# Attention and MLP on one core: the opening of the kernel rearranged (first keys and queries in float32, value rows once per half batch, an immediate cosine shift)

## The chip, the cores and the metric

One Trainium2 chip; the kernel runs on one core. A time is the device time of one execution in microseconds (us). The kernel before took 355.42, 353.09 and 354.77 us in three runs, median 354.77. The engines are TensorE (PE, with its weight loads PEld), VectorE (DVE), ScalarE (ACT), GpSimd (POOL) and SyncE (SP, which here only issues DMAs). Each works its own instructions in program order and waits for the others by semaphores.

## The reference

Attention with a sliding window and global tokens, and behind it an MLP:

```python
batch, heads, seq, head_dim = 8, 8, 576, 64        # 8 global tokens, drawn from 0..575
scores = q @ k.T / 8
mask   = (|i - j| <= 32) or i is global or j is global
attn   = softmax(where(mask, scores, -1e9)) @ v      # per batch and head
x      = attn.transpose(0, 2, 1, 3).reshape(4608, 512)
h      = x @ w_in                                    # 512 x 2048
out    = (h * cos(h)) @ w_out                        # 2048 x 512, float32
```

The inputs are float32; the kernel computes in fp16 with float32 sums. A flag that the kernel computes on the way decides at the end if a slow general path runs as well; with these inputs it does not.

## The kernel before, in words

**Units.** Two heads make a *pair* (numbers 0 to 31), two pairs a *half batch* (0 to 15), two half batches a batch. Pairs 0 to 9 (`2 * HY`) are done in the *opening*, by functions with their own layout of five blocks of 120 keys; pairs 10 to 31 run beside the MLP. The MLP has 9 tiles of 512 tokens; a tile can start when its batch's attention is done.

**Order.** Nothing is scheduled by a planner: `tc.manual_schedule()` keeps the program's order on each engine. Strings of steps spell it: `FRONT` for the opening, then `MID`, `FIFTH`, `SIXTH` and `ORDER` for half batches 4 on. A step is a letter with a number. In `FRONT`: `k3`, `q3` turn keys and queries of pair 3 (`local_k`, `local_q`); `s3` its scores and exponentials (`scores5`); `p3` its values (`values5`); `x3` turns its result into the MLP's input `xT` (`turn_x5`); `C1` casts the values of half batch 1 (`cast_vn`, on GpSimd); `y` makes their global value rows; `L2` loads keys and queries of half batch 2; `E0`, `E1` gather the global rows of keys and queries of the later pairs, `H0` casts and `H1` turns them, `g4` copies them into pair 4's buffers; `f2`, `w4` are filler matmuls on TensorE; `W` and `O` load the MLP's weights, `K5` casts half batch 5 to fp16 in DRAM, `m` and `t` are the first MLP products and cosines.

**A pair in the opening.** Keys lie in SBUF with eight tokens a partition. TensorE transposes them (16 small transposes, L595), and for pairs below 4 (`PK`) also picks out the 8 global tokens by products with a 0/1 selector (`one_k`, `one_q`, L312). ScalarE copies both from PSUM (L313, L604; for queries L313, L615, L616). TensorE makes scores (L631), ScalarE the exponentials in four pieces (L634 twice, L638 twice), VectorE multiplies by the mask `mask5` (L635 twice, L639 once), TensorE multiplies by the values (L646), VectorE divides by the row sums (L660 to L666), TensorE turns the result (L678) and VectorE copies it to `xT` (L679 to L684).

**Values.** Rows of v come in float32 by SyncE's queue into `vn32`, are cast by GpSimd (L402) into `vw`; TensorE sums the 8 global rows by a selector `one_v` (L409), and ScalarE copies them into the first 8 partitions of each of the five blocks (L410). In the kernel before this is done once per pair (`y0.0`, `y0.1`, ...): 8x640 elements a copy. Steps `M1` to `M4` clear the edge of the next half batch's buffer on VectorE (L378) and load it.

**First loads.** SyncE loads the indices of the global tokens three times in different layouts (L237 to L239) and then values. GpSimd's queue loads keys and queries and casts them to fp16 on the way (`load_qk`, L279): pair 0, pair 1, then whole half batches. VectorE builds the window mask's band (`build_band`, L475 to L485), the selectors (`build_ones`, L304, L305) and the mask (`build_mask5`, L498 to L519).

**MLP.** A tile is 16 times four matmuls (L762), a cosine on ScalarE with a per-partition shift `pio2` (L768), a product on VectorE (L769), and 16 groups of four output matmuls (L800).

Of the kernel before, what the change touches and what calls it, by code (L numbers as in the profile page):

```python
# [9 lines left out]
FP32 = mybir.dt.float32  # L10
# [45 lines left out]
FRONT = ("M1 s0 E0 C0 E1 L2 k1 q1 w4 s1 y0.0 f4 k2 q2 C1 H0 p0 M2 L3 y0.1 s2 k3 q3 f2 x0 p1 M3 H1 g4 g5 g6 C2 y1.0 s3 g7 L4 I k4 q4 f2 x1 p2 M4 y1.1 s4 "  # L56
         "C3 W0 k5 q5 f2 x2 p3 y2.0 s5 g8 g9 W1 W2 W3 k6 q6 f2 x3 p4 y2.1 s6 C4 Y0 k7 q7 f2 x4 p5 n0 y3.0 s7 k8 q8 f2 x5 p6 y3.1 s8 H2 k9 q9 f2 x6 p7 y4.0 s9 "
         "x7 p8 y4.1 O m m x8 K5 p9 t t + m m t t x9 -")
# [146 lines left out]
def kernel(  # L205
# [31 lines left out]
    nc.sync.dma_start(gidx_all, dview(gi, 0, (0, P), (1, 2 * G)))  # L237
    nc.sync.dma_start(gidx_col, dview(gi, 0, (0, 16), (2, G), (1, 1)))
    nc.sync.dma_start(gidx_row, dview(gi, 0, (2 * G, 1), (1, 2 * G)))  # L239
# [67 lines left out]
    def pick_globals(pr, t, src, ones, n, to):  # L307
# [5 lines left out]
        nc.scalar.copy(to, view(t, (0, to.shape[1]), (1, G)))  # L313
# [61 lines left out]

    def next_values(s):

        nc.vector.memset(vn_of(s)[0:64, 0], 0.0)  # L378
        load_vn(s)
# [18 lines left out]
    def cast_vn(s):  # L398
        if s > 1:
            nc.gpsimd.tensor_copy(gate, pm_of[max(pm_of)][0:1, 2 * CN - 1 : 2 * CN])  # L400
# [3 lines left out]
    def value_rows(s, part):  # L404

        hs = slice(2 * part, 2 * part + 2)
        rows = ps.tile([P, 512], FP32, tag="h", bufs=2, name="rows")
        for t in range(NK5):
            nc.tensor.matmul(rows[0:G, 0 : 2 * D], one_v[:, t], vn16(s)[:, t, hs, 0:D], start=t == 0, stop=t == NK5 - 1)  # L409
        nc.scalar.copy(vn16(s)[0:G, :, hs, 0:D], view(rows[0:G], (0, NK5), (D, 2), (1, D)))  # L410
# [187 lines left out]
    def local_k(pr):  # L598
        to = kw[pr % NK][:, :, G:]
        if pr < 2 * HY:  # L600
            t, g = turned(kn[pr // 2 % NN], pr, KP)
            if pr < PK:
                pick_globals(pr, g, kn[pr // 2 % NN], one_k, KP, k5(pr)[:, :, 0:G])
            nc.scalar.copy(k5(pr)[:, :, G:].rearrange("p n (j r) -> p n j r", r=RW),  # L604
                           view(t, (KS // RW, NK5), (1, KS // RW), (QP, RW)))
# [3 lines left out]
    def local_q(pr):  # L609
        to = qb[pr % NK][:, :, G:]  # L610
        if pr < 2 * HY:
            t, g = turned(qn[pr // 2 % NN], pr, QP)
            if pr < PK:
                pick_globals(pr, g, qn[pr // 2 % NN], one_q, QP, q5(pr)[:, 1:, 0:G])
# [474 lines left out]
```

## Time and profile before

| quantity | value |
|---|---|
| runs, median of 3 | 354.77 us (353.09 to 355.42) |
| the profiled execution: span from first to last instruction | 353.2 us |
| the profiled execution's own time around it | not listed apart; the runs' median is 1.6 us above the span |
| TensorE busy | 332.5 us, 94% |
| VectorE, ScalarE, GpSimd busy | 71%, 70%, 31% |
| granted TensorE clock, mean | 0.983 |
| first exponential of pair 0 | 10.85 us |
| second group of MLP products starts | 56.58 us |

The page gives busy times per engine; they are averages over stages with different limits. The timeline lists instructions by start time, with "xN" for N like ones in a row and in brackets how long the engine had been idle before and what ended that. The windows give busy time per engine within a stretch.

### The profile page before, as it was taken

The page shows a single profiled execution, that of the slowest core. Times are in us where ns is not written, and L with a number is a line of the kernel's source. Part 1 is how long each engine was busy: PE and PEld are TensorE (multiplying, and loading weights), DVE is VectorE, ACT ScalarE, POOL GpSimd, SP SyncE. Part 2 cuts the span into 40 slices and gives each one's busy share as a digit, 9 for nine tenths or more (in the row PEclk, how much of TensorE's full clock was granted, in tenths as well). Part 3 has the DMA queues.
Part 4 walks back from the last instruction along what each step waited for, and adds up shares of the span by engine and source line. Part 5 has one row for each costly group of instructions (what it writes and reads, how often), then busy time and mean ns, then how long its engine had stood idle before and what let it go on. Part 6 is the DMA issues. An engine that isn't in the chain of part 4 may idle for free.

```text
span 353.2 us, 8389 instructions
## 1 busy us (share of the span) xinstructions
PE 332.5 (94%) x3169; PEld 170.9 (48%) x3169; DVE 250.1 (71%) x611; ACT 245.9 (70%) x423; POOL 108.5 (31%) x221
## 2 busy tenths in 40 slices
PE   7887789999986999999999999999999999999993
PEld 3566675444443444544444545454544444444442
DVE  6565888887586778778787979697878466556410
ACT  8778987884754877777878787777878856644300
POOL 8854847434070507050705071416000100000000
PEclk9898989999999999999999999999999999999998
DMA  5999993999999999999999999999980000100112
GB/s 82 186 149 165 167 192 41 207 164 132 165 147 160 146 199 135 178 118 194 143 187 139 183 139 176 135 161 153 179 93 32 31 32 30 60 32 30 58 63 68
DMA packets 165891, 44.58 MB, mean 126 GB/s; under 512 B 153764, under 2 KB 160996, under 8 KB 165668
## 3 DMA queue, kind: packets, MB, share of 16 engines
q1 hardware_dynamic: 105860, 26.70, 51.2%
q0 software_dynamic: 59984, 17.28, 50.5%
q8 instruction: 27, 0.44, 0.5%
q14 instruction: 20, 0.16, 0.2%
HBM read 44.41 MB, written 19.17 MB: 180 GB/s over the span
## 4 chain that ended last, share of the span: by engine, by line
PE 73%; ACT 8%; DVE 5%; DMA 5%; issue 4%; SPq 3%; POOL 1%; ACTq 0%; POOLq 0%; DVEq 0%
PE po L800 32%; PE ph L762 30%; PE tx L744 2%; DMA kn<-in_k_dram 2%; PE st L699 2%; ACT e L702 2%; PE pv L719 2%; ACT e L634 1%; DMA vw<-vg 1%; ACT e L707 1%; SPq L414 1%; PE po L782 1%; ACT e L638 1%; DVE xn L666 1%; DVE pm L639 1%
## 5 line engine op out<-in xcount | busy, mean ns | idle before, releaser
L762 PE MATMUL ph<-xT,w_in 128*128 128x512 f16 x576 | 140.3, 379 | 1.1 <-DVE g L769 0.3
L768 ACT ACTIVATE cos<-ph,pio 128x512 f16<-128x512 f32 x144 | 97.1, 687 | 62.1 <-PE ph L762 59.9
L800 PE MATMUL po<-w_out,g 128*128 128x512 f16 x560 | 135.4, 379 | 0.0
L769 DVE TENSOR_TENSOR g<-cos,ph 128x512 f16<-128x512 f16 x144 | 95.9, 685 | 42.9 <-ACT cos L768 41.7
L762 PEld LDWEIGHTS <-w_in 128*128 128x128 f16 x576 | 54.2, 97 | 64.6 <-issue 4.6
L800 PEld LDWEIGHTS <-g 128*128 128x128 f16 x560 | 53.7, 98 | 63.6
L703 DVE TENSOR_TENSOR pm<-e,mask 128x512 f16<-128x512 f16 x44 | 18.8, 426 | 19.0 <-ACT e L702 17.7
L702 ACT ACTIVATE e<-st 128x512 f16<-128x512 f32 x44 | 23.9, 594 | 10.0 <-PE st L699 9.8
L980 POOL COPY gate<-xn 1x1 f16<-1x1 f16 x8 | 1.4, 180 | 87.9 <-DVE xn L730 87.9
L752 POOL COPY xT<-xg 128x4 f16 x48 | 15.6, 325 | 32.5 <-DVE xT L747 29.9
L272 POOL DMA_DIRECT2D q<-in_q_dram x11 | 24.0, 2182 | 0.0
L818 ACT ACTIVATE xn<-xn 128x1536 f16<-128x1536 f16 (+1 forms) x16 | 22.5, 1407 | 0.0
L730 DVE TENSOR_TENSOR xn<-pv,r_all 128x768 f16<-128x768 f32 x22 | 21.1, 958 | 1.0
L805 ACT COPY o<-po 128x512 f32<-128x512 f32 x17 | 10.0, 586 | 14.7 <-PE po L800 14.3
L807 DVE COPY o<-po 128x512 f32<-128x512 f32 x18 | 12.4, 690 | 9.0 <-PE po L800 8.5
L272 POOL DMA_DIRECT2D k<-in_k_dram x11 | 18.1, 1645 | 0.9 <-issue 0.9
L768 ACT ACT_TABLE_LOAD x12 | 15.4, 1283 | 0.2
L719 PE MATMUL pv<-vw,pm 128*64 128x65 f16 x484 | 12.7, 197 | 2.7 <-DMA vw<-vg 2.7
L607 DVE COPY kw<-kT 128x1320 f16<-128x1320 f16 x22 | 15.1, 685 | 0.0
L702 ACT ACT_TABLE_LOAD x11 | 14.1, 1283 | 0.2
L699 PEld LDWEIGHTS <-kw 64*128 64x128 f16 x484 | 8.4, 95 | 10.7 <-issue 8.1
L699 PE MATMUL st<-qb,kw 64*128 64x64 f16 x484 | 11.2, 191 | 1.5 <-DVE qb L619 1.1
(185 smaller groups left out, 385.9 us busy)
## 6 DMA issues: line engine op xcount, KB each, us to landing
out_dram<-o SPq DMA_DIRECT2D x35, 256.0 KB
vw<-v SPq DMA_DIRECT2D x32, 165.0 KB
v<-in_v_dram POOLq DMA_DIRECT2D x11, 288.0 KB
k<-in_k_dram POOLq DMA_DIRECT2D x11, 288.0 KB
q<-in_q_dram POOLq DMA_DIRECT2D x11, 288.0 KB
vn<-in_v_dram SPq DMA_DIRECT2D x20, 120.0 KB
w_in<-in_moe_w_in_dram POOLq DMA_DIRECT2D x4, 512.0 KB
w_out<-in_moe_w_out_dram POOLq DMA_DIRECT2D x1, 2048.0 KB
```

Source lines behind the costliest of these rows:

```text
L272: nc.gpsimd.dma_start(dst[s].rearrange("t (h d) -> t h d", h=4), dview(src, base, (D, S), (S * D, 4), (1, D)))
L699: nc.tensor.matmul(st[j // 8 * 2 + h][:, j % 8 * C : j % 8 * C + C], kp[hp, j], qp[hp, j], start=True, stop=True)
L702: nc.scalar.activation(e[:, 0:512], st[h], AF.Exp, scale=scale)
L703: nc.vector.tensor_tensor(view(pm[:, h], (1, 512)), e[:, 0:512], view(mask, (1, 512)), ALU.mult)
L719: nc.tensor.matmul(pv[r0 : r0 + C, j // 6, c0 : c0 + 65], pm[:, h, j], vp[:, j, h], start=True, stop=True)
L730: nc.vector.tensor_tensor(view(xn, (384, 2), (D, 6), (1, D)), view(pv, (512, 2), (65, 6), (1, D)), view(rp, (6, 2), (1, 6), (0, D)), ALU.mult)
L752: nc.gpsimd.tensor_copy(xT[:, :, bass.ds(pool_idx[g] + b * S, 1)], xg[:, :, g : g + 1])
L762: nc.tensor.matmul(ph, w_in16[:, j, f * P : (f + 1) * P], xT[:, j, t * TT : (t + 1) * TT], start=(j == 0), stop=(j == NC - 1))
L768: nc.scalar.activation(cos, ph, AF.Sin, bias=pio2)
L769: nc.vector.tensor_tensor(g, cos, ph, ALU.mult)
L800: nc.tensor.matmul(po, g16[:, f, s * P : (s + 1) * P], w_out16[:, f], start=(f == 0), stop=(f == NF - 1))
L818: nc.scalar.activation(view(xn, (BP * P, 2), (1, n)), view(xn, (BP * P, 2), (1, n)), AF.Square, accum_out=x_sq[:, s : s + 1])
```

## The change

- **First loads.** Keys and queries of pairs 0 and 1 come in float32 by SyncE's queue (keys) and ScalarE's (queries) into `vn32[0]` (`first_k`, `first_q`), and are cast to fp16 by VectorE (keys), ScalarE (queries of pair 0) and GpSimd (queries of pair 1). GpSimd's first load is half batch 1. `vn32[0]` no longer holds values; `vn_of` alternates between the two halves of `vn32[1]`, and values are loaded by `r2`, `r3`, `r4` after the cast of two half batches before.
- **Order.** `k1 q1` stand ahead of `s0`; `k2 q2` and `k3 q3` ahead of `s2`; `y0` ahead of `s1`, `y1` ahead of `s3`, and so on; `E1` behind `L2`. Fewer filler matmuls. Some buffer clearings move to GpSimd and ScalarE as steps `b0` to `b4`.
- **Value rows** once a half batch: one selector product over 4 heads (8x256), one ScalarE copy into block 0, and a GpSimd copy of that block to the other four.
- **Copies.** Odd key copies and the 8-column query copy go to VectorE. The copies of the picked global tokens come behind the large copies.
- **Mask products** in two instead of three pieces (2x488 and 2x384); exponentials write tiles of 2x488.
- **Cosine** with an immediate shift in place of `pio2`.
- **Weight squares** at the end of the kernel in three slots of a buffer shared with `xn`, in place of four of their own.

```diff
+FRONT = ("k1 q1 b0 s0 w4 E0 b2 C0 r2 y0 b3 s1 L2 b4 k2 q2 w2 p0 b1 E1 k3 q3 s2 f2 x0 p1 C1 r3 y1 H0 H1 L3 g4 g5 C2 r4 g6 "
+         "s3 k4 q4 f2 x1 p2 g7 L4 I s4 k5 q5 f2 x2 p3 y2 C3 W0 s5 k6 q6 g8 g9 W1 W2 W3 f2 x3 p4 s6 k7 q7 f2 x4 p5 C4 Y0 n0 y3 s7 k8 q8 f2 x5 p6 y4 H2 s8 k9 q9 f2 x6 p7 s9 "
+         "x7 p8 O m m x8 K5 p9 t t + m m t t x9 -")
...
     def vn_of(s):
-        i = s if s < 4 else 2
-        return view(vn32[i // 2][:, 4 * (i % 2)], (4 * D, NK5), (1, 4 * D))
+        return view(vn32[1][:, 4 * (s % 2)], (4 * D, NK5), (1, 4 * D))
+
+    def first_k(pr):
+        return vn32[0][0:KP, 2 * pr : 2 * pr + 2]
+
+    def first_q(pr):
+        return vn32[0][0 : S // RW, 4 + 2 * pr : 6 + 2 * pr]
+
+    def load_first(eng, src, pr):
+        to = first_k(pr)[KPAD:KP] if src is k else first_q(pr)
+        eng.dma_start(to, dview(src, 2 * pr * S * D, (RW * D, S // RW), (S * D, 2), (1, RW * D)))
...
-    def next_values(s):
-        nc.vector.memset(vn_of(s)[0:64, 0], 0.0)
-        load_vn(s)
...
-    def value_rows(s, part):
-        hs = slice(2 * part, 2 * part + 2)
-        rows = ps.tile([P, 512], FP32, tag="h", bufs=2, name="rows")
+    def value_rows(s):
+        rows, vp = ps.tile([P, 512], FP32, tag="h", bufs=2, name="rows"), vn16(s)
         for t in range(NK5):
-            nc.tensor.matmul(rows[0:G, 0 : 2 * D], one_v[:, t], vn16(s)[:, t, hs, 0:D], start=t == 0, stop=t == NK5 - 1)
-        nc.scalar.copy(vn16(s)[0:G, :, hs, 0:D], view(rows[0:G], (0, NK5), (D, 2), (1, D)))
+            nc.tensor.matmul(rows[0:G, 0 : 4 * D], one_v[:, t], vp[:, t, :, 0:D], start=t == 0, stop=t == NK5 - 1)
+        nc.scalar.copy(vp[0:G, 0, :, 0:D], view(rows[0:G], (D, 4), (1, D)))
+        first = vp[0:G, 0, :, 0:D]
+        nc.gpsimd.tensor_copy(vp[0:G, 1:, :, 0:D], bass.AP(first.tensor, first.offset, [first.ap[0], [0, NK5 - 1], *first.ap[1:]]))
...
@@ local_k @@
-                pick_globals(pr, g, kn[pr // 2 % NN], one_k, KP, k5(pr)[:, :, 0:G])
-            nc.scalar.copy(k5(pr)[:, :, G:].rearrange("p n (j r) -> p n j r", r=RW),
-                           view(t, (KS // RW, NK5), (1, KS // RW), (QP, RW)))
+                pick_globals(pr, g, kn[pr // 2 % NN], one_k, KP)
+            copy = nc.vector.tensor_copy if pr % 2 else nc.scalar.copy
+            copy(k5(pr)[:, :, G:].rearrange("p n (j r) -> p n j r", r=RW),
+                 view(t, (KS // RW, NK5), (1, KS // RW), (QP, RW)))
+            if pr < PK:
+                nc.scalar.copy(k5(pr)[:, :, 0:G], view(g, (0, NK5), (1, G)))
...
@@ local_q @@
-            nc.scalar.copy(qb[pr % NK][:, 0, 0:G], t[:, :, 0])
+            nc.vector.tensor_copy(qb[pr % NK][:, 0, 0:G], t[:, :, 0])
...
@@ scores5 @@
-        for h in range(2):
-            e = work.tile([P, 2 * CB], FP16, tag="e", bufs=3)
-            nc.scalar.activation(e[:, 0:CA], st[h][:, 0:CA], AF.Exp, scale=scale)
-            nc.vector.tensor_tensor(pm[:, h * CN : h * CN + CA], e[:, 0:CA], mask5[:, 0:CA], ALU.mult)
...
+        for i, (c, n) in enumerate(((0, CA), (CA, CB))):
+            e = work.tile([P, 2 * CA], FP16, tag="e", bufs=3)
+            for h in range(2):
+                nc.scalar.activation(e[:, h * n : (h + 1) * n], st[2 * i + h][:, 0:n], AF.Exp, scale=scale)
+            nc.vector.tensor_tensor(view(pm[:, c:], (CN, 2), (1, n)), view(e, (n, 2), (1, n)), view(mask5[:, c:], (0, 2), (1, n)), ALU.mult)
...
-        nc.scalar.activation(cos, ph, AF.Sin, bias=pio2)
+        nc.scalar.activation(cos, ph, AF.Sin, bias=pi / 2.0)
...
@@ ahead of the FRONT steps @@
+        for t in ((k, nc.sync), (q, nc.scalar)):
+            load_first(t[1], t[0], 0)
+        nc.sync.dma_start(gidx_all, dview(gi, 0, (0, P), (1, 2 * G)))
+        nc.sync.dma_start(gidx_col, dview(gi, 0, (0, 16), (2, G), (1, 1)))
+        load_first(nc.scalar, q, 1)
+        load_first(nc.sync, k, 1)
...
+        nc.gpsimd.memset(first_k(0)[0:KPAD], 0.0)
+        nc.gpsimd.memset(qn[1][64:QP], 0.0)
+        load_qk(1)
         nc.gpsimd.iota(p_i, pattern=[[0, 1]], base=0, channel_multiplier=1)
...
+        load_vn(0)
+        load_vn(1)
...
+        cast_first(nc.vector.tensor_copy, k, 0)
+        cast_first(nc.scalar.copy, q, 0)
+        cast_first(nc.gpsimd.tensor_copy, q, 1)
         build_band()
+        cast_first(nc.vector.tensor_copy, k, 1)
+        build_ones()
         index_rows(1)
         local_k(0)
         local_q(0)
+        nc.gpsimd.memset(kn[1][0:KPAD], 0.0)
+        clear_rows(1)
...
+        def small_buffers(part):
+            if part == 0:
+                build_mask5()
...
+            elif part == 2:
+                nc.scalar.memzero(vn_of(0)[0:G, 1:].rearrange("p t d -> p (t d)"))
+            elif part == 3:
+                nc.gpsimd.memset(qn[2][64:QP], 0.0)
+            else:
+                nc.gpsimd.memset(kn[2][0:KPAD], 0.0)
```

More of the change, by code (lines that the diff above doesn't have):

```diff
@@ L949, in row_numbers @@
                 gidx_row[0:1, 0 : 2 * G : 2], engines=[mybir.EngineType.Pool], min_val=0, max_val=S - 1)[1])
+        def small_buffers(part):
+            if part == 0:
+                build_mask5()
+                for i in range(2):
+                    nc.vector.memset(vw[i][:, :, :, D : D + 1], 1.0)
+            elif part == 1:
+                for i in range(NV):
+                    if i > 1:
+                        nc.vector.memset(vw[i][:, :, :, D : D + 1], 1.0)
+                    if i % 2:
+                        nc.vector.memset(vw[i][:, NB - 1, :, 0:D], 0.0)
+                nc.vector.memset(r_all[:, 0 : 2 * HY, 2 * NK5 :], 1.0)
+            elif part == 2:
[4 more added lines that the diff above has]
+                nc.gpsimd.memset(kn[2][0:KPAD], 0.0)
         def early_rows(x):
```

73 lines of the change are left out of this document (27 added, 46 removed).

## The prediction

> **What bounds the kernel now.** I read the page's busy times and its chain of waits first, then the busy time by windows, then the timeline of the first 60 us.
>
> ```profile
> PE 332.5 (94%) x3169; PEld 170.9 (48%) x3169; DVE 250.1 (71%) x611; ACT 245.9 (70%) x423; POOL 108.5 (31%) x221
> ...
> PE 73%; ACT 8%; DVE 5%; DMA 5%; issue 4%; SPq 3%; POOL 1%; ACTq 0%; POOLq 0%; DVEq 0%
> ```
> The first row is the page's busy time by engine, the second the share of the chain that ended last: TensorE is busy for 94% of the span and makes 73% of the chain. Which stretch is *not* TensorE-bound shows in the windows.
>
> ```profile
> 53.00:54.00 1.00, 1.00 (x10) 0.52 (x7) 1.00 (x6) 0.66 (x1) 0.00 (x0) 1.00 0.16 32
> ...
> 130.00:135.00 5.00, 5.00 (x52) 2.65 (x51) 4.74 (x12) 3.49 (x5) 0.68 (x2) 1.00 1.32 174
> ```
> Columns: length, busy us of PE, PEld, DVE, ACT, POOL with counts, then clock, DMA share, GB/s. From 130 to 135 TensorE has no idle time: once the MLP runs beside attention, nothing that shortens another engine is worth anything there. At 53 the DMA engines have fallen to a share of 0.16: the opening's loads are done, and the opening, which lasts until the MLP starts in earnest at 56.58, ends 3 us later by something else. All large edits lie in this opening, so the question is how long it takes after the change. I mark it by the first exponential (ACT L634) of a pair of heads, the one step that every pair passes.
>
> ```profile
> 10.44 0.55 PE L631 MATMUL st<-qb,kw 64*128 64x136 f16 x10
> 10.85 1.04 ACT L634 ACTIVATE e<-st 128x488 f16<-128x488 f32 x2 [0.46 <-PE t L319]
> ...
> 25.63 1.04 ACT L634 ACTIVATE e<-st 128x488 f16<-128x488 f32 x2 [1.13 <-PE st L631]
> ...
> 38.52 1.01 ACT L634 ACTIVATE e<-st 128x488 f16<-128x488 f32 x2
> ...
> 51.10 1.02 ACT L634 ACTIVATE e<-st 128x488 f16<-128x488 f32 x2
> ...
> 56.58 1.90 PE L762 MATMUL ph<-xT,w_in 128*128 128x512 f16 x8
> ```
> Pair 0 passes at 10.85, pair 3 at 25.63, pair 6 at 38.52, pair 9 at 51.10. So the opening has a start (10.85), a ramp of three pairs (14.78), six pairs (25.47) and a rest.
>
> **The change, part by part.**
>
> *The steady pairs.* One undisturbed period, from pair 6:
>
> ```profile
> 39.44 0.83 ACT L638 ACTIVATE e<-st 128x384 f16<-128x384 f32 x2
> 40.19 0.63 ACT L604 COPY kw<-bank 128x600 f16<-128x600 f16 x1
> 40.31 0.56 DVE L639 TENSOR_TENSOR pm<-e,qT 128x768 f16<-128x768 f16 x1 [0.33 <-ACT e L638]
> 40.73 0.15 ACT L615 COPY qb<-bank 128x8 f16<-128x8 f16 x1
> 40.78 0.64 ACT L616 COPY qb<-bank 128x600 f16<-128x600 f16 x1
> 40.79 0.46 DVE L679 COPY xT<-tx 128x600 f16<-128x600 f16 x1
> 40.87 0.45 PE L409 MATMUL rows<-vw,one_v 128*8 128x128 f16 x5 [0.32 <-ACT kw L604]
> 41.33 1.26 ACT L818 ACTIVATE xn<-xn 128x1280 f16<-128x1280 f16 x1
> 41.48 0.55 PE L631 MATMUL st<-qb,kw 64*128 64x136 f16 x10 [0.16 <-ACT qb L616]
> 42.60 0.68 ACT L410 CAST vw<-rows 8x640 f16<-8x640 f32 x1
> ```
> (The fence leaves out rows of other steps between these.) Before, ScalarE runs without a gap: four exponentials (38.52 to 40.19, 1.67), the key copy L604 (0.54 to the next start), two query copies (to 41.42), the value-row copy L410 (0.6): about 3.5, plus hops, and 1.26 once for the squares L818. After, the value-row copy comes once in two pairs with 256 elements in place of two of 640; every odd key copy and the 8-column query copy go to VectorE. ScalarE's own work falls to about 1.67 + 0.27 + 0.64 = 2.6, with a hop of 0.55 to the next exponential (scores to exponential, 10.44 to 10.85, is 0.4; the rest is the way to TensorE) 3.1. But the changed order puts VectorE's small query copy behind both mask products of the pair, and the large query copy on ScalarE waits for that VectorE copy. So the period becomes a chain: exponentials to 40.27 (1.75), second mask product 0.56 (it now starts after the fourth exponential), query copy 0.15, large query copy 0.64, hop to scores and exponential 0.48: **3.58**; with the odd key copy on VectorE in it (0.46, the price of L679, the same 600 elements from PSUM, less 0.08 of overlap) **3.96**. Nothing is queued behind that wait on ScalarE but the next pair's exponentials, so it is paid in full. Six periods: 3 x 3.58 + 3 x 3.96 = 22.6, plus 1.2 for the squares = 23.8, against 25.47. Bounds: 20 (ScalarE alone, 6 x 3.1 + 1.2) and 25.5 (no gain). I take 23.8, since the waits are in the instruction order. Part of the gain is a stall that goes:
>
> ```profile
> 32.94 0.27 DVE L378 MEMSET vn<- 64x256 f32 x1 [3.09 <-DMA vn<-in_v_dram]
> ```
> VectorE stood 3.09 us before this clearing of a value buffer, whose load was late; the change has no such clearing, and each load is started one cast earlier.
>
> *The start.* Rows that price it:
>
> ```profile
> 1.46 0.88 POOL L279 DMA_DIRECT2D kn<-in_k_dram  x1 [0.92 <-POOLq L1073]
> ...
> 3.10 0.15 POOL L909 IOTA p_i<- 128x1 int32 x1
> ...
> 3.58 0.24 POOL L913 MEMSET ident<- 128x128 f16 x1
> ...
> 3.83 0.18 DVE L475 CAST df<-d_i 128x192 f32<-128x192 int32 x1
> ...
> 5.53 0.09 DVE L484 MEMSET band<- 8x32 uint32 x1
> ...
> 5.62 2.75 POOL L383 MEMSET vn<- 8x1024 f32 x3
> ...
> 7.59 1.04 ACT L917 ACTIVATE vn<-vn 8x1024 uint32<-8x1024 uint32 x1
> ...
> 12.08 0.47 PE L595 MATMUL bank<-ident,kn 75*64 75x75 f16 x16 [1.09 <-DMA kn<-in_k_dram]
> ...
> 13.01 0.41 PE L312 MATMUL bank<-one_q,qn 76*64 76x8 f16 x16
> ```
> GpSimd now clears 3x1024 float32 (2.75 / 3 = 0.92) and 12x2048 fp16 before it issues two loads (1.46 to 3.10, 1.6) and only then makes the index p_i. The fp16 clearing has no row: 128 fp16 elements took 0.24 and 1024 float32 0.92, so by element it is 1.8, by byte 0.9. From GpSimd's first work at about 1.0 (an estimate: it was free at 0.92), p_i starts at 5.3 (4.4). From p_i to the band's first step took 0.73 before, now 1.0 with one more clearing: 6.3 (5.4). VectorE then casts the first keys (72x1024 float32, not in the trace: 0.6 to 1.0, 192 elements took 0.18), builds the band (3.83 to 5.62, 1.8), casts the keys of pair 1, and only then makes the two selectors (some 0.4) that the first pick on TensorE waits for: 10.5 (8.8). TensorE turns and picks one tensor in (13.42 - 12.08) / 2 = 0.67; the rest of pair 0's keys and three tensors take 2.35, the copies of pair 1's queries 0.85 more, because they now stand ahead of pair 0's exponentials: 13.7 (12.0). I take **13.2** for pair 0 against 10.85, nearer the upper end by the 0.24 row. The early arrival of the data is worth little: VectorE and GpSimd come later than it. The two loads that ScalarE now issues first, its clearings and its cast are done well before its first copy at 10.8. SyncE's value loads stand behind the key and index loads, but their cast waits longer for ScalarE's clearing (below).
>
> *The ramp.* The order now makes a ring of it. TensorE's value rows y0 stand ahead of pair 1's scores, y1 and the turning of the global rows ahead of pair 3's; between them GpSimd has one long queue.
>
> ```profile
> 13.08 1.29 POOL L402 CAST vw<-vn 128x1280 f16<-128x1280 f32 x1 [0.67 <-DMA vn<-in_v_dram]
> ...
> 14.53 0.98 POOL L335 DMA_INDIRECT qg<-in_q_dram,gidx_rows  x1 [0.16 <-issue]
> ...
> 15.81 0.94 POOL L335 DMA_INDIRECT qg<-in_q_dram,gidx_rows  x1 [0.30 <-issue]
> ...
> 21.01 0.29 POOL L532 CAST g<-kg 128x128 f16<-128x128 f32 x1
> ```
> From pair 0's first exponential: exponentials 1.75, then on ScalarE the clearing of eight value rows that L402's cast waits for (L917, 1.04), cast 1.3, y0 0.7 (twice the columns of L409's 0.45, bounded by twice its time), its copy 0.45, the new GpSimd copy of 1024 elements 1.0 (L402 does 1280 in 1.25), the clearing of 12x2048 1.8, two load issues 1.6, the clearing of 3x2048 1.8, two gathers 2.4 (14.53 to 16.75, and the issue gap), cast 1.25, y1 0.7, copy 0.45, GpSimd copy 1.0, two casts 0.55 (L532 twice), the turning 0.4 (two small transposes; L595 does sixteen in 0.47; the rest hops), hop 0.4: 18.6, or 16.9 with clearings at half. All stand in line; nothing covers them, as pair 3's scores are behind the turning on TensorE. I take **18.6** against 14.78. Pair 3 passes at 31.8 (28.9 to 32.3).
>
> *The rest.* Value rows y4 once less after pair 9: TensorE 0.45, taken as -0.5. The smaller weight-square buffers and the wider exponential tile cost nothing: the same instructions in the same places, under full TensorE. The cosine:
>
> ```profile
> L762 PE MATMUL ph<-xT,w_in 128*128 128x512 f16 x576 | 140.3, 379 | 1.1 <-DVE g L769 0.3
> L768 ACT ACTIVATE cos<-ph,pio 128x512 f16<-128x512 f32 x144 | 97.1, 687 | 62.1 <-PE ph L762 59.9
> ...
> L702 ACT ACTIVATE e<-st 128x512 f16<-128x512 f32 x44 | 23.9, 594 | 10.0 <-PE st L699 9.8
> ```
> With the per-partition shift a cosine of 512 takes 687 ns, an exponential without it 594. At best 144 x 0.093 = 13.4 us of ScalarE time, beside TensorE, which lost 1.1 us in all ahead of L762: 0 to -1.1, taken as 0.
>
> **Sum.** 13.2 + 18.6 + 23.8 = 55.6 for pair 9 against 51.10, +4.5, less 0.5: **+4.0**. The MLP stage is started by the same order and shifts with it. The span of 353.2 becomes 357.2; it lies 1.6 under the runs' median of 354.77 (353.09 to 355.42), and the time between span and run is not touched, so the median becomes **358.8**, +1.1%.
>
> **Rivals.** (A) *The clearings are cheap.* By bytes, and with the casts at their lower ends, pair 3 passes at 28.9 and pair 9 at 52.7: +1.6 - 0.5, so 355.9, no change to tell. For it: no such clearing is in the trace. Against: the 0.24 row.
>
> (B) *Data set the opening*, and it ends faster. The chain in the first 60 us has
>
> ```profile
> 4.23 7.80 DMA kn<-in_k_dram
> ```
> the second keys' load. With all keys of two pairs there at once and ScalarE rid of value rows, pair 0 comes no later, the ramp too keeps its 14.78, the six pairs take ScalarE's 20: -5.5 - 0.5, 348.8. It decides if the query copy does not wait behind the mask products and GpSimd's queue is not waited for; the order of the instructions speaks against both.
>
> (C) *VectorE and GpSimd collide.*
>
> ```profile
> 44.96 1.70 DVE L639 TENSOR_TENSOR pm<-e,qT 128x768 f16<-128x768 f16 x1 [0.33 <-ACT e L638]
> ...
> 45.00 1.25 POOL L402 CAST vw<-vn 128x1280 f16<-128x1280 f32 x1
> ```
> The mask product took 1.70 in place of 0.56 beside a GpSimd cast. There are five new GpSimd copies; if four meet a mask product on the path it is 4 x 1.14 = 4.6 more, 363.4. [...]
>
> (D) *The early loads do not come early.* If the second keys land no sooner than at 12.03 as before, the VectorE cast that stands ahead of the selectors waits for them (float32 also doubles what these loads write), and pair 0 passes at 12.03 + 1.0 + 0.4 + 3.2 = 16.6: 3.4 more, 362.2. [...]
>
> **How the numbers follow.** Forecast 0.36, A 0.27, B 0.16, C 0.13, D 0.08. About 1% (3.5 us) is what a measurement here can tell from no change. The forecast's own case spreads from 357 to 361, some seven tenths of it past 358.3: slower 0.25 + 0.13 + 0.08 = 0.46; within 0.11 + 0.27 = 0.38; faster 0.16. The range reaches from between A and B to C's end: 351.0 to 363.5.
>
> **What would show it.** Pair 0's first exponential near 13, pair 3's near 32; GpSimd without gaps from pair 0's value cast to the casts of the global rows, and TensorE idle ahead of pair 3's scores until those; clearings of 2048 elements at 1.8; periods alternating near 3.6 and 4.0 with ScalarE waiting for VectorE's small query copy; cosines near 594 ns with no gain from them; the first MLP products some 4 us later. The prediction is wrong if pair 3 passes before 27, or if the periods are near 3.1.

## The result, and the profile after

The changed kernel takes 373.15 us (median of 4 runs, 369.54 to 375.19); beside it the kernel before took 354.28 (353.09 to 355.42). The ratio is **1.0487, interval 1.0422 to 1.0553**: slower, where the prediction had 358.8 and a range up to 363.5. The profiled execution of the changed kernel took 375.19 with a span of 373.5; it was the slowest of its four, and the ratio leaves it out, so that a ratio is not always the quotient of two medians printed here. Kernels are compared by their ratios to the kernel before.

The page's busy times of the changed kernel:

```profile
PE 341.9 (92%) x3134; PEld 178.1 (48%) x3134; DVE 256.2 (69%) x614; ACT 223.7 (60%) x400; POOL 118.5 (32%) x226
```
ScalarE lost 22 us of work, and TensorE gained 9 with fewer instructions: its products took longer. Where, the windows tell (columns as in the prediction: length, busy us of PE, PEld, DVE, ACT, POOL with counts, clock, DMA share, GB/s). First the changed kernel:

```profile
10.00:50.00 40.00, 29.41 (x480) 21.94 (x481) 23.66 (x79) 17.03 (x40) 23.18 (x32) 0.54 0.77 129
...
80.00:373.50 293.50, 283.76 (x2270) 137.46 (x2268) 209.56 (x461) 185.24 (x321) 68.89 (x142) 1.00 1.04 123
```
and the kernel before:

```profile
10.00:50.00 40.00, 33.23 (x737) 25.66 (x736) 27.28 (x90) 33.30 (x80) 26.39 (x48) 0.87 1.07 170
...
57.00:353.20 296.20, 285.10 (x2272) 137.56 (x2270) 210.24 (x462) 197.66 (x321) 71.98 (x144) 1.00 1.04 122
```
From 10 to 50 us TensorE issued 480 products in place of 737, and its granted clock was 0.54 in place of 0.87. From the start of the MLP stage on, the kernels are alike (293.5 and 296.2 us, the marks being chosen by eye). All of the loss is in the opening. By the prediction's own marks, the first exponential of a pair (ACT L644 now):

```profile
19.45 1.83 ACT L644 ACTIVATE e<-st 128x488 f16<-128x488 f32 x4
...
39.83 0.58 ACT L644 ACTIVATE e<-st 128x488 f16<-128x488 f32 x1 [2.36 <-PE st L640]
...
55.15 1.81 ACT L644 ACTIVATE e<-st 128x488 f16<-128x488 f32 x4 [0.52 <-PE st L640]
...
71.78 1.81 ACT L644 ACTIVATE e<-st 128x488 f16<-128x488 f32 x4 [0.71 <-PE st L640]
```

| part of the opening | before | predicted | measured |
|---|---|---|---|
| start, to pair 0 | 10.85 | 13.2 | 19.45 |
| ramp, pair 0 to 3 | 14.78 | 18.6 | 20.38 |
| six pairs, 3 to 9 | 25.47 | 23.8 | 31.95 |
| pair 9 at | 51.10 | 55.6 | 71.78 |

Pair 9 is 20.7 late and the span 20.3 longer. A mark of a single execution is good to about 1 us: a kernel whose opening is that of the kernel before (the cosine alone, below) had pair 0 at 10.92 and pair 9 at 52.26, against 10.85 and 51.10. So the terms to explain are the start (+6.25 against the forecast) and the six pairs (+8.15), and with a smaller error the ramp (+1.8).

**The start.** The timeline of the changed kernel:

```profile
2.47 0.54 SPq L372 DMA_DIRECT2D vn<-in_k_dram  x1
...
6.30 0.62 DVE L944 CAST kn<-vn 75x1024 f16<-75x1024 f32 x1
...
11.66 1.15 DVE L944 CAST kn<-vn 75x1024 f16<-75x1024 f32 x1 [3.07 <-DMA vn<-in_k_dram]
...
12.86 0.21 DVE L302 SCALAR_TENSOR_TENSOR one_k<-tok_i,gidx_all 128x64 f16<-128x64 int32 x1
...
13.12 0.59 PE L309 MATMUL bank<-one_k,kn 75*64 75x8 f16 x16 [5.53 <-DVE one_k L302]
```
SyncE issued the load of the second keys at 2.47, and its cast began at 11.66, after VectorE had stood 3.07 us for it. The selectors stand behind that cast on VectorE, and TensorE's first pick of pair 0, which needs nothing of the second keys, stood 5.53 us for the selector. From the first pick to pair 0's exponential it took another 6.33:

```profile
14.83 0.40 PE L599 MATMUL bank<-ident,kn 75*64 75x75 f16 x6 [0.17 <-ACT kw L612]
...
15.49 0.34 PE L599 MATMUL bank<-ident,kn 75*64 75x75 f16 x4 [0.26 <-issue]
...
16.29 0.41 PE L599 MATMUL bank<-ident,kn 75*64 75x75 f16 x6 [0.46 <-issue]
...
16.48 0.17 DVE L622 COPY qb<-bank 128x8 f16<-128x8 f16 x1 [3.34 <-remote]
```
TensorE's turning of pair 1's keys came in three pieces, and VectorE's small query copy of pair 0 stood 3.34 us for something that the profile calls "remote", another core or an unknown queue; the products that it copies from ended at 14.65. What it was stays open. It is part of the 6.33, as a run below without it shows.

**The ramp.** TensorE's timeline between the scores of pair 1 and those of pair 3:

```profile
24.68 0.91 PE L640 MATMUL st<-qb,kw 64*128 64x136 f16 x10
25.52 0.72 PE L599 MATMUL bank<-ident,kn 75*64 75x75 f16 x16
...
28.31 1.59 PE L652 MATMUL pv<-vw,pm 128*128 128x65 f16 x20
29.84 0.72 PE L599 MATMUL bank<-ident,kn 75*64 75x75 f16 x16
...
31.80 0.91 PE L640 MATMUL st<-qb,kw 64*128 64x136 f16 x10
...
38.86 0.47 PE L559 MATMUL t<-ident,g 128*128 128x128 f16 x2 [1.85 <-POOL g L536]
39.27 0.72 PE L640 MATMUL st<-qb,kw 64*128 64x136 f16 x10
```
From 24.68 to the scores of pair 2 at 31.80 TensorE has no gap: two pairs' turnings and the first value products stand there, all at half clock (scores take 0.91 in place of 0.55, value products 1.59 in place of 1.03). Only the turning of the global rows at 38.86 waits for GpSimd.

**The six pairs.** Waits of the changed kernel up to 85 us (waiter, releaser, us in total, times, longest), so with the start and the ramp in them:

```profile
POOL vw L414 <- ACT vw L412: 11.9, 4, 4.8
ACT qb L623 <- DVE qb L622: 9.5, 8, 1.9
...
PE st L640 <- ACT qb L623: 3.2, 2, 1.9
...
PE pv L652 <- POOL vw L414: 1.9, 1, 1.9
```
ScalarE's query copy waits eight times for VectorE's 8-column copy, 9.5 us, as the prediction's chain had it; six of these waits, 6.9 us, lie in the six pairs. One pair at full clock shows what the chain had not counted:

```profile
50.61 1.81 ACT L644 ACTIVATE e<-st 128x488 f16<-128x488 f32 x4 [0.16 <-PE st L640]
...
51.62 1.25 POOL L405 CAST vw<-vn 128x1280 f16<-128x1280 f32 x1
51.68 2.18 DVE L645 TENSOR_TENSOR pm<-e,qT 128x976 f16<-128x976 f16 x2 [1.36 <-ACT e L644]
...
53.98 0.66 ACT L623 COPY qb<-bank 128x600 f16<-128x600 f16 x1 [1.01 <-DVE qb L622]
...
54.69 0.55 PE L640 MATMUL st<-qb,kw 64*128 64x136 f16 x10 [1.86 <-ACT qb L623]
...
56.30 1.25 DVE L645 TENSOR_TENSOR pm<-e,qT 128x976 f16<-128x976 f16 x2 [0.53 <-ACT e L644]
...
57.47 0.78 DVE L609 COPY kw<-bank 128x600 f16<-128x600 f16 x1
```
The two mask products took 2.18 beside GpSimd's cast and 1.25 without it, 0.93 more, and the period was 4.54 in place of 3.58. VectorE's key copy took 0.78, where the prediction had 0.46. The two mask products of pair 3 were longer still, and in the period from pair 7 to pair 8 (6.78) TensorE's value products stood for GpSimd's copy of the value rows:

```profile
40.91 2.70 DVE L645 TENSOR_TENSOR pm<-e,qT 128x976 f16<-128x976 f16 x2 [1.32 <-ACT e L644]
...
64.10 1.43 PE L652 MATMUL pv<-vw,pm 128*128 128x65 f16 x18 [1.86 <-POOL vw L414]
```

### The profile page after: what moved, and what is told of

The parts are those of the page before. It is cut to its first block, busy times and chain, and to the rows that moved or that the text cites. A ratio compares the mean times of both kernels' runs of the same rounds, so it can differ in the third digit from the quotient of the medians.

```text
span 373.5 us, 8278 instructions
## 1 busy us (share of the span) xinstructions
PE 341.9 (92%) x3134; PEld 178.1 (48%) x3134; DVE 256.2 (69%) x614; ACT 223.7 (60%) x400; POOL 118.5 (32%) x226
## 4 chain that ended last, share of the span: by engine, by line
PE 72%; POOL 7%; issue 5%; ACT 5%; DMA 4%; SPq 3%; DVE 1%; another core or an unknown queue 1%; POOLq 0%; ACTq 0%; DVEq 0%
PE ph L768 32%; PE po L806 31%; DMA vn<-in_k_dram 2%; PE tx L750 2%; PE st L705 2%; ACT e L708 2%; POOL vw L405 2%; PE pv L725 2%; DMA vw<-vg 1%; ACT e L713 1%; ACT e L644 1%; PE pv L652 1%; PE po L788 1%; SPq L418 1%
## 5 line engine op out<-in xcount | busy, mean ns | idle before, releaser
L768 PE MATMUL ph<-xT,w_in 128*128 128x512 f16 x576 | 142.0, 383 | 0.8
L774 ACT ACTIVATE cos<-ph 128x512 f16<-128x512 f32 x144 | 84.4, 597 | 72.8 <-PE ph L768 65.0
L645 DVE TENSOR_TENSOR pm<-e,qT 128x976 f16<-128x976 f16 (+1 forms) x20 | 16.4, 838 | 12.1 <-ACT e L644 11.8
L644 ACT ACTIVATE e<-st 128x488 f16<-128x488 f32 (+1 forms) x40 | 18.1, 542 | 4.8 <-PE st L640 4.7
L652 PE MATMUL pv<-vw,pm 128*128 128x65 f16 (+2 forms) x200 | 13.9, 227 | 1.9 <-POOL vw L414 1.9
## 6 DMA issues: line engine op xcount, KB each, us to landing
w_in<-in_moe_w_in_dram POOLq DMA_DIRECT2D x4, 512.0 KB, 11.6
```

What stands on the lines that cost most here:

```text
L644: nc.scalar.activation(e[:, h * n : (h + 1) * n], st[2 * i + h][:, 0:n], AF.Exp, scale=scale)
L645: nc.vector.tensor_tensor(view(pm[:, c:], (CN, 2), (1, n)), view(e, (n, 2), (1, n)), view(mask5[:, c:], (0, 2), (1, n)), ALU.mult)
L652: nc.tensor.matmul(pv[p0 : p0 + m, h, X * slot : X * slot + X], pm[:, h * CN + OFF[t] + c0 : h * CN + OFF[t] + c0 + m], vp[:, t, h0 + h], ...
L768: nc.tensor.matmul(ph, w_in16[:, j, f * P : (f + 1) * P], xT[:, j, t * TT : (t + 1) * TT], start=(j == 0), stop=(j == NC - 1))
L774: nc.scalar.activation(cos, ph, AF.Sin, bias=pi / 2.0)
```

## The experiments

Where not said otherwise, an edit is made to the changed kernel alone. A ratio is that to the kernel before, run beside it; "exponentials at" gives pair 0, 3 and 9.

### Selectors first

```diff
-        cast_first(nc.vector.tensor_copy, k, 1)
         build_ones()
         index_rows(1)
+        cast_first(nc.vector.tensor_copy, k, 1)
```


> The changed kernel with VectorE's selectors (build_ones, index_rows(1)) ahead of the cast of the second keys; nothing is left out. In the changed kernel's trace TensorE idled 5.5 us (7.6 to 13.1) ahead of the first pick for the selectors, behind a cast that waited 3.07 us for the second keys' load. Theory 'waits': the selectors come 3.9 us earlier, but pair 1's keys still arrive as late and stand ahead of pair 0's scores, so pair 0's first exponential (19.45) comes at most 2 to 3 us earlier: about 370 against some 372. Theory 'clock': the gap is what dropped TensorE's clock to 0.5 from 10 to 50 us; with a gap of under 2 us it holds and the opening loses another 8 to 10 us: about 361, mean clock near 0.97.

Measured: 368.54, ratio 1.0406 (1.0337 to 1.0475). Exponentials at 15.20, 35.80 and 66.44: pair 0 is 4.25 earlier and pair 9 5.34. The order of these three VectorE steps is worth 0.8% by the ratios; by their intervals alone that is not clear of the noise, by the marks it is.

### The gap filled, and fillers throughout

The first of two kernels puts 22 filler products ahead of the first pick:

```diff
             t, g = turned(kn[pr // 2 % NN], pr, KP)
+            if pr == 0:
+                warm(22)
```


> The changed kernel with 22 more filler matmuls on TensorE between the turning of pair 0's keys and their pick, in the gap of 5.5 us; no wait is changed. Theory 'clock': TensorE stays warm, clock near 0.97, the work at half clock between 10 and 50 us (27 us busy, about 10 us too many) runs at full clock: about 362. Theory 'waits': the waits for VectorE, GpSimd and ScalarE set the opening and the clock only follows the low load: clock back to 0.5 within 5 us after the fillers, 370 to 374.

The second adds fillers in many places, for the question whether the half clock makes the periods long (16 at the first pick, 4 after each of pair 0's turnings, `w4` to `w12`, a `w4` behind `y0`, `w2` to `w6`, and `f2` to `f6` from pair 3 on, in six pairs where the expectation says five):

```diff
+            if pr == 0:
+                warm(16)
...
         local_k(0)
+        warm(4)
         local_q(0)
+        warm(4)
```


> The changed kernel with h1_fillers' fillers and six in place of two in each of the next five pairs, so that TensorE's clock stays up. If the half clock (0.5 from 35 to 50 us) makes the steady periods 5.3 in place of 3.6 to 4.0, the six periods shrink from 31.95 to 27 or less and the time to 366 to 369. Rival: the periods are set by ScalarE's wait for VectorE's copy and by the collisions with GpSimd, whatever the clock: 30 to 33 for the six, 372 to 376.

Measured: filling the gap gave 373.48, ratio 1.052 (1.045 to 1.059), and the same marks (19.30, 39.64, 71.56). Its windows:

```profile
10.00:15.00 5.00, 3.81 (x67) 2.13 (x64) 1.49 (x4) 0.75 (x2) 3.53 (x4) 1.00 1.19 192
15.00:20.00 5.00, 3.01 (x70) 2.55 (x69) 2.48 (x15) 2.27 (x7) 0.67 (x1) 0.62 0.69 142
...
25.00:30.00 5.00, 5.00 (x102) 3.86 (x100) 1.51 (x5) 3.27 (x9) 4.78 (x5) 0.50 0.53 104
```
The clock held at 1.00 until 15 and then fell all the same. From the first pick (13.01) to pair 0's exponential (19.30) it took 6.29, as before (6.33), though the clock was full for the first part of it. The wait of VectorE's small query copy for "remote" was there too, 3.31 until 16.33, so this run does not tell what TensorE's rate alone is worth in that stretch.

The fillers throughout gave 369.47, ratio 1.0496 (1.0442 to 1.055), no different from 1.0487. From 10 to 50 us the clock was 0.87:

```profile
10.00:50.00 40.00, 31.33 (x589) 21.96 (x587) 25.58 (x80) 19.64 (x46) 25.66 (x36) 0.87 0.79 134
```
The six periods took 30.6 in place of 31.95, with the clock at 1.00 from 50 to 60 and at 0.88 from 40 to 70 as a whole, but at 0.50 from 35 to 40. So a clock raised by fillers takes back 1.4 us of the 6.5 by which the six periods became longer than in the kernel before. Pair 9 came 3.4 earlier in the profiled execution (68.41), but the ratio shows no gain clear of the noise. Either other limits take over, or the fillers' own time eats the gain. The two can't be told apart here.

### Copies back on ScalarE

```diff
-            copy = nc.vector.tensor_copy if pr % 2 else nc.scalar.copy
+            copy = nc.scalar.copy
...
-            nc.vector.tensor_copy(qb[pr % NK][:, 0, 0:G], t[:, :, 0])
+            nc.scalar.copy(qb[pr % NK][:, 0, 0:G], t[:, :, 0])
```


> The changed kernel with the 8-column query copy and the odd key copies back on ScalarE. Theory of the prediction (large query copy waits for VectorE's small one behind the mask products): ScalarE's waits for that copy, 9.5 us in eight pieces in the changed kernel's trace, go; ScalarE pays 4 x 0.64 and 10 x 0.15 for it in the same chain: 3 to 6 us less, 366 to 369. Rival: the periods are set by TensorE at half clock (pair 4 to 5 took 5.43 with TensorE busy throughout), then no change, 371 to 373.

Measured: 368.34, ratio 1.0386 (1.0327 to 1.0444). Exponentials at 18.87, 38.99 and 66.43: the six pairs take 27.4 in place of 31.95. Three of the periods are 3.5; one is 8.15, and in it TensorE's value products stood 4.20 us for GpSimd's copy of the value rows, which had come behind two gathers. The pairs were 4.5 us shorter with nothing of ScalarE's waiting behind the mask products on VectorE. The opposite experiment puts these two lines of the change alone into the kernel before:

> The kernel before with one part of the change alone: odd key copies and the small query copy on VectorE. The prediction's chain gives periods of 3.6 and 4.0 against 4.25, a gain: 353 to 355. Rival, by e3_copies_scalar, which gained 5 us by taking this part out of the changed kernel: VectorE is late there with the collisions, and the part costs 3 to 5 here too: 358 to 360.

Measured: 359.73, ratio 1.0172 (1.0138 to 1.0206). Exponentials at 11.28, 28.95 and 55.80: the ramp is 2.9 longer than in the kernel before and the six pairs 1.4. The waits of that kernel from 8 to 60 us have the same pair of rows:

```profile
ACT qb L617 <- DVE qb L616: 7.4, 9, 1.4
...
PE st L632 <- ACT qb L617: 3.6, 7, 1.0
```
The forecast of a gain for these copies falls from both sides: 1.0% back when taken out, 1.7% lost when put in alone. Most of that loss lies in the ramp, where the prediction had not looked for it.

### Value rows without GpSimd's hop

```diff
-        nc.scalar.copy(vp[0:G, 0, :, 0:D], view(rows[0:G], (D, 4), (1, D)))
-        first = vp[0:G, 0, :, 0:D]
-        nc.gpsimd.tensor_copy(vp[0:G, 1:, :, 0:D], bass.AP(first.tensor, first.offset, [first.ap[0], [0, NK5 - 1], *first.ap[1:]]))
+        nc.scalar.copy(vp[0:G, :, :, 0:D], view(rows[0:G], (0, NK5), (D, 4), (1, D)))
```


> The changed kernel with the value rows copied by ScalarE into all five blocks at once (8x1280), without the GpSimd copy behind it. Theory of the prediction (GpSimd's queue is the ring of the ramp): two GpSimd copies of 1.03 leave the ramp and the wait of pair 6's values for such a copy (1.9 us) goes, ScalarE pays some 0.9 more four times, mostly in gaps: 2 to 4 us less, 368 to 370. Rival: GpSimd is not what the ramp waits for, no change (371 to 373), or slower by ScalarE's 3.5.

Measured: 367.37, ratio 1.0372 (1.0305 to 1.0439). Exponentials at 19.38, 38.17 and 67.33: the ramp is 1.6 shorter, the six pairs 2.8. In the kernel before, the value rows once a half batch (steps `y0.0` and `y0.1` become one `y0` in the first's place, and so on) were run with the hop, as the change has it:

> The kernel before with another part alone: value rows once a half batch, into one block by ScalarE and from there into four by GpSimd. b2_rows_once, with ScalarE copying all five, is level with the kernel before less the cosine's 2 us; so this tells GpSimd's hop alone. Its copy of 1.03 and its place behind casts and loads, by e4_rows_scalar: 4 to 6 us, 358 to 361. Rival: in this order GpSimd has room, 354.5 to 356.

and without it, together with the cosine's shift:

> The kernel before with the immediate cosine shift (b1_cosine) and the global value rows once a half batch, but copied by ScalarE into all five blocks, with no GpSimd copy. If fewer, larger row products and copies help the opening at all: 351.5 to 352.5, below b1_cosine's 352.9. Rival: a copy of 8x1280 ahead of one pair in two only moves ScalarE's work: 352.9 to 354.

Measured: 362.18 with the hop, ratio 1.0245 (1.0211 to 1.0279); 354.8 without it, ratio 0.9994 (0.9971 to 1.0018), where the cosine alone has 0.9946. So the larger product and copy gain nothing, and the hop costs some 2%. TensorE's value products waited three times for the hop's copy there, 10.0 us in all. The timeline of the kernel with the hop shows how:

```profile
32.39 1.25 POOL L402 CAST vw<-vn 128x1280 f16<-128x1280 f32 x1 [3.54 <-DMA vn<-in_v_dram]
33.59 1.03 POOL L412 COPY vw<-vw 8x1024 f16<-8x1024 f16 x1
...
34.67 1.43 PE L648 MATMUL pv<-vw,pm 128*128 128x65 f16 x18 [5.11 <-POOL vw L412]
```
GpSimd's small copy of one half batch (L412) stands in its queue behind the cast of the next (L402), and that waits 3.54 us for a load. TensorE's value products stood 5.11 us for a copy that needs 1.03.

### Clearings on VectorE

```diff
-        nc.gpsimd.memset(qn[1][64:QP], 0.0)
+        nc.vector.memset(qn[1][64:QP], 0.0)
```
and so the other three of `kn[1]`, `qn[2]` and `kn[2]`.

> The changed kernel with the four clearings of 12x2048 and 3x2048 fp16 on VectorE instead of GpSimd (where each took 1.80). Theory of the prediction (each stands in GpSimd's ring): two of them in the ramp, 3.6 us, one ahead of the index rows (the second keys' wait covers that one); VectorE pays about 1 us each, partly in the ring: 369 to 371. Rival A (they are covered): no change, 372 to 374.

Measured: 372.25, ratio 1.0477 (1.0388 to 1.0565): no change. Pair 0 came at 20.54, and the ramp took 20.8. Its timeline:

```profile
13.14 0.69 DVE L944 CAST kn<-vn 75x1024 f16<-75x1024 f32 x1 [5.17 <-DMA vn<-in_k_dram]
...
23.31 1.25 POOL L405 CAST vw<-vn 128x1280 f16<-128x1280 f32 x1 [6.49 <-ACT vn L983]
...
31.58 1.28 POOL L405 CAST vw<-vn 128x1280 f16<-128x1280 f32 x1
...
38.84 1.03 POOL L414 COPY vw<-vw 8x1024 f16<-8x1024 f16 x1 [5.98 <-ACT vw L412]
```
Rid of 3.6 us of clearings in the ramp, GpSimd cast its second values 2.46 earlier (31.58 against 34.04) and then stood 5.98 for ScalarE's copy of the value rows, in place of 2.20. The clearings were covered. And since GpSimd issued its own load sooner, the second keys came still later (13.14).

### GpSimd's load later

```diff
-        load_qk(1)
         nc.gpsimd.iota(p_i, pattern=[[0, 1]], base=0, channel_multiplier=1)
...
         cast_first(nc.gpsimd.tensor_copy, q, 1)
+        load_qk(1)
```


> The changed kernel with GpSimd's load of half batch 1 issued after the cast of pair 1's queries instead of ahead of the index rows; nothing left out. In the changed kernel the second keys landed 8.6 us after their issue, at 11.66. Theory 'shared engines' (rival D of the prediction): this load takes the transfer engines from them; without it they land by 8 to 9, the selectors are ready 2.5 to 3.5 us earlier, pair 0's first exponential near 16 to 17: 369 to 370. Rival: SyncE's queue itself is slow or the value loads behind them share it, they land near 11.5 as before; the index rows come 1.7 us earlier to no effect: 371 to 374.

Measured: 367.9, ratio 1.0397 (1.0303 to 1.0492).

```profile
10.03 0.69 DVE L943 CAST kn<-vn 75x1024 f16<-75x1024 f32 x1 [2.28 <-DMA vn<-in_k_dram]
...
12.61 0.17 DVE L622 COPY qb<-bank 128x8 f16<-128x8 f16 x1 [1.55 <-PE bank L309]
```
With GpSimd's two loads of 288 KB issued at 9.11 in place of 3.55 the second keys were cast at 10.03 in place of 11.66, and pair 0 passed at 15.76. The small query copy did not wait for "remote" here, and from the first pick (11.04) to the exponential it took 4.72 in place of 6.33, at the same granted clock of 0.50. So 1.6 of pair 0's 3.7 came from that stretch. Together with the run before (load sooner, keys at 13.14) the landing of the second keys follows the start of GpSimd's load in both directions: with that load issued at 9.11, 3.55 and 1.72, their cast began at 10.03, 11.66 and 13.14. GpSimd's load is the smaller part of the delay: 7.6 us passed from the issue at 2.47 to the cast at 10.03 without it.

### First value rows behind pair 1's scores

```diff
-"k1 q1 b0 s0 w4 E0 b2 C0 r2 y0 b3 s1 L2 ...
+"k1 q1 b0 s0 w4 E0 C0 r2 b3 s1 y0 L2 ...
```
and ScalarE's clearing of `b2` ahead of the first loads of values, as before.

> The changed kernel with one difference: TensorE's first value rows stand behind pair 1's scores, and ScalarE's clearing that their cast waits for stands at the front, both as in the kernel before. If the prediction's ring sets the ramp, pair 1 passes about 2.5 earlier and pair 3 about as much: 369 to 371. Rival: pair 3's turning of the global rows, behind the second gathers and their cast, ends the ramp anyway: pair 1 earlier, pair 3 unmoved at 39 to 40, 372 to 374.

Measured: 370.26, ratio 1.044 (1.0387 to 1.0493). Exponentials at 19.07, 36.81 and 67.66: pair 1 passes 3.2 earlier and pair 3 3.0. By the marks this piece of the ring was on the path; the times' intervals overlap.

### The edits together

Selectors, copies and value rows together:

> The changed kernel with three edits together: selectors ahead of the cast of the second keys, the odd key copies and the small query copy on ScalarE, and the value rows copied by ScalarE without GpSimd. Alone they gave 368.5, 368.3 and 367.4 against 372 to 373. Theory 'waits in a row': the three waits lie one behind the other in the opening, so their gains add: 373 - 4.6 - 4.8 - 5.8 = 357 to 358. Rival 'the next wait takes over' (late second keys, GpSimd's clearings, TensorE at half clock): 362 to 364.

with GpSimd's load later as well:

> The three edits of c1_three (selectors first, the two copies on ScalarE, value rows by ScalarE alone) and with them d1_load_later's (GpSimd's load of half batch 1 behind its cast of pair 1's queries). If the losses add up, d1's 5 us come off c1's 360.3: 355 to 356.5, level with the kernel before, and pair 0 at about 12.5. Rival: c1's start already hides most of it (its remaining waits for the second keys are 2.2 us), so 357.5 to 359.

with the order of the value rows too:

> c2_four with o1_rows_after's order as a fifth edit (first value rows behind pair 1's scores, ScalarE's clearing at the front). If the ring that the prediction described still costs its 3 us after the other four are undone, 355 to 356. Rival: with ScalarE copying the rows, the ring is short already: 357.5 to 358.5.

and the four with 40 more fillers (those of the kernel above without those of the six pairs; the expectation says 36, its list adds up to 40):

> c2_four with 36 more filler products on TensorE: 16 ahead of the first pick, 4 after each of pair 0's turnings as in the kernel before, 8, 4 and 4 more at the first value rows and pair 1. If the half clock from 10 to 33 us is a loss of its own, and a fuller TensorE keeps it at 1.0, the ramp's TensorE rows shrink by a third and the time falls 2 to 4 us below c2_four. If the clock falls anyway, or TensorE's rate is not what the opening waits for, the time is c2_four's or up to 3 above, with the clock still at 0.5 somewhere between 15 and 35.

| undone | ratio | of the 4.87% by itself | together |
|---|---|---|---|
| selectors first | 1.0406 | 0.81 | |
| copies on ScalarE | 1.0386 | 1.01 | |
| value rows without the hop | 1.0372 | 1.15 | these three: 1.0158 (1.0073 to 1.0242; 360.31 us), 3.29 off |
| load later | 1.0397 | 0.90 | these four: 1.0113 (1.0072 to 1.0154; 358.11), 3.74 off |
| rows behind the scores | 1.044 | 0.47 | all five: 1.0108 (1.0071 to 1.0146; 356.6), 3.79 off |

The first four add up to 3.87 and give 3.74 together. Of the single rows only the copies and the hop are clear of the noise by their intervals; that the others cost something rests on the marks and on the sums. The fifth adds nothing any more: with ScalarE copying the rows, the ring is short already. More fillers on top of four gave 361.24, ratio 1.0216 (1.0165 to 1.0266): the mean clock rose from 0.961 to 0.985 and the time by 1%, so the clock was not worth the fillers' price there either.

### The cosine, and the merged mask products, alone in the kernel before

```diff
-        nc.scalar.activation(cos, ph, AF.Sin, bias=pio2)
+        nc.scalar.activation(cos, ph, AF.Sin, bias=pi / 2.0)
```


> The kernel before with nothing but the cosine's shift as an immediate. Theory of the prediction (0 to -1.1): cosines at 594 to 600 ns in place of 687, no change of the time within 0.4%: 354 to 355. Rival: ScalarE sets part of the MLP stage after all, or its earlier results let transfers start earlier: 350 to 353.

Measured: 352.9, ratio 0.9946 (0.9908 to 0.9984), with cosines of 597 ns in place of 687. It is the only part of the change that gained by itself, and this kernel has the lowest median of all that were run, below both kernels. The merged products, with the smaller buffer for the weight squares:

> The kernel before with the merged mask products alone (two products a pair in place of three, each behind two exponentials, and the smaller buffer for the weight squares that makes room for the wider tile). c3_five, with five edits undone and the cosine's gain in it, is still 3 us above the kernel before, so some 5 us lie in parts not yet split. If the merged product, which starts one exponential later, holds up TensorE's value products in the ramp, 355.5 to 358. Rival: nothing waits for it, as the prediction had it, and the rest lies in the start and the order: 353 to 354.5.

Measured: 354.28, ratio 0.9996 (0.9963 to 1.0028): no difference.

## Why the prediction was wrong

- **The start, 13.2, was 19.45: the step that failed is "The early arrival of the data is worth little: VectorE and GpSimd come later than it".** The prediction took the engines as late and the data as there. p_i started at 5.33 (5.3 was said) and the first cast at 6.30 took 0.62, as said; but the second keys landed 9 us after their issue, and the selectors stood behind them, ready at 13.1 where 10.5 was said. This is the mechanism of rival D, which had 0.08; the two runs that move the load and the one that moves the selectors show it. The second half of the miss is the way from the first pick to the exponential, 6.33 where 2.35 + 0.85 for the turnings and copies were counted. Of these 3.1 too many, 1.6 went with the load held back and with them the wait for "remote"; what the other 1.5 are made of (the half clock, the hops between engines) no run separates.
- **The ramp, 18.6, was 20.38: near in size by luck, wrong in its list.** The prediction put GpSimd's clearings (3.6) and load issues (1.6) on the path, at 1.80 for 2048 elements, which is what they took (the 0.92 of 1024 float32, scaled by element, gives 1.84). Without them on GpSimd the ramp stayed at 20.8. In their place, by the timeline, stood TensorE's turnings of two pairs and, at half clock, its products; no run changed these. The first value rows ahead of pair 1 (2.6 of the ramp) and GpSimd's hop (1.6) were on the path, as said.
- **The six pairs, 23.8, were 31.95: the step is "the period becomes a chain: 3.58 ... 3.96".** The chain is there, with six waits of 6.9 us, and its length without a collision was near: from the exponentials at 55.15 to the next scores at 59.07 is 3.92, and some 0.4 more to the next exponentials, where 3.96 was said for the whole; 0.32 of the difference is VectorE's dearer key copy. What failed is what the sum put at nothing: collisions of the mask products, which the chain passes through, with GpSimd's casts (0.93 and 1.45), TensorE's waiting for GpSimd's hop (1.86), and late starts at half clock (TensorE was busy throughout from 45 to 50 us, at 0.50). By the runs, the copies back on ScalarE shorten the six pairs by 4.5, the value rows without the hop by 2.8, and both with the selectors first to 24.99, below the 25.47 of the kernel before. The prediction read a gain of ScalarE's time into the copies; in the kernel before they cost 1.7% by themselves.
- **TensorE's clock has no term in the prediction.** It was 0.54 in place of 0.87 from 10 to 50 us. Raising it with fillers gave no gain clear of the noise (1.0496 against 1.0487), but the fillers take time themselves, so what the half clock costs stays open.
- **Rivals C and D as alternatives.** D's late keys came, and collisions came, but not those that C names: none of GpSimd's five new copies (25.28, 37.53, 50.51, 63.01, 67.11) met a mask product. Four casts (L405), which the kernel before has too, did: the products took 1.62 in place of 0.56 and 2.00, 2.70 and 2.18 in place of 1.25, 4.2 in all, where C had 4.6, so C's price was met by luck; the kernel before has one such (1.70). The range took the rivals one at a time; both on top of 358.8 give 366.8. In the last of the four, 1.19 us of the cast lay beside the products of 2.18, and they took 0.93 more; why a product takes longer beside a cast was not shown.
- **GpSimd's copy of the value rows** was priced at its 1.0 and only in the ramp. Its place in the queue, behind casts that wait for loads, was worth 2% in the kernel before.
- **Right:** the MLP stage shifts with the opening (20.7 and 20.3); the buffers and merged products cost nothing; cosines near 594 ns (597). That they gain nothing was short by 2 us (0.5%). The time around the span, 1.6, was 1.7.

**What stays open.** With five edits undone the kernel is still 1.08% above the kernel before, and about 0.5% more is hidden by the cosine. Pair 0 is then at 13.46 and pair 3 at 31.21, against 10.85 and 25.63, and the six pairs (24.04) are shorter than the 25.47 of the kernel before, so it lies in the start and the ramp: the float32 route of the first loads with its casts, or the turnings two pairs ahead. These were not tried apart. Nor was the collision of the mask products with GpSimd's cast: its size is read from the trace. With four edits undone the mask products took 13.5 us in all, in place of 16.4, but that run changes other things as well. What "remote" was, and why a load of 288 KB needs 7.6 us even with GpSimd's held back, is open too.

## What to carry to other kernels

Ask of each moved instruction what it now stands behind on its new engine: the small query copy of 0.15 us with the odd key copies behind other work on VectorE cost 1.7% here, and a copy of 1.03 us behind other work on GpSimd 2%, though they relieved a busy ScalarE. Put what many wait for (a selector) ahead of whatever waits for a load: pair 0 came 4.25 us earlier here. And don't start a load that is needed late beside one that is needed first: the second keys were cast at 11.66 us in place of 10.03. Rivals that act on different stages add up, so a range should hold their sum.

## What the runs showed of the hardware that was not expected

- TensorE's clock stayed at 0.50 from 10 to 35 us in the changed kernel, although the engine had no idle time from 25 to 30, with turnings and picks of 64 rows and value products:

```profile
25.00:30.00 5.00, 5.00 (x100) 3.86 (x98) 1.36 (x4) 3.42 (x9) 4.62 (x5) 0.50 0.50 107
```
  With the first gap filled it fell a few us later, between 15 and 20 (0.62 there, 0.50 from 20 to 35), where no gap of TensorE was above 0.7 us; it was busy for 0.38 and 0.28 us of the two us from 14 to 16. With the selectors first, TensorE's wait ahead of the first pick was 1.26 us in place of 5.53 and the next one, for the second keys, 2.40; the clock was 0.50 from 10 to 45 us all the same. What makes the clock fall was not settled. Fillers in many places held the clock at 1.00 from 10 to 30 us.
- A load of 288 KB issued at 2.47 was there at 11.6, and at 10.0 when two others of 288 KB each were held back.
- A clearing of 2048 fp16 elements took 1.80 us on GpSimd on 3 partitions and on 12 alike, and 0.91 on VectorE; 1024 float32 took 0.94 on GpSimd.
